# Clustered attention and max-out feed-forward on one core: the exponential left in PSUM for every second score tile

## The chip, the cores and the metric

The kernel runs on one NeuronCore of one Trainium2 chip. The core has a matrix engine (TensorE, PE in the rows; its weight loads are PEld), a vector engine (VectorE, DVE), a scalar engine (ScalarE, ACT), a general engine (GpSimd, POOL) and a queue that issues the transfers (SyncE, SP). SBUF is the working memory of 128 partitions; PSUM is the matrix engine's result memory, 8 banks of 512 float32 values in each partition. POOL does not touch PSUM in this kernel; DVE and ACT read it. The metric is device time of one execution in microseconds (us).

## The reference

Shapes: `q`, `k`, `v` are (4 batches, 8 heads, 768 positions, 64), there are 16 centroids per head, and the feed-forward takes 3072 tokens of 512 through 768 hidden columns.

```python
q_assign = argmax(einsum('bhsd,hcd->bhsc', q_n, c_n), axis=-1)
k_assign = argmax(einsum('bhsd,hcd->bhsc', k_n, c_n), axis=-1)
mask = q_assign[:, :, :, None] == k_assign[:, :, None, :]
scores = where(mask, scale * matmul(q, k.transpose(0, 1, 3, 2)), -1e9)
scores = scores - max(scores, axis=-1, keepdims=True)
attn = exp(scores)
attn = attn / (sum(attn, axis=-1, keepdims=True) + 1e-9)
x = matmul(attn, v)                      # then to [3072, 512]
h = maximum(maximum(x @ w1, x @ w2), x @ w3)
out = h @ w_out
```

## The kernel before

**Precision.** Every float32 operand of a large product is held as two float16 parts, a high half (the rounded value) and a low half (value minus high half). A product is then three matmuls: high by high, high by low and low by high. The inputs are scaled by powers of two first; for queries and keys of a pair of heads the factor to scale the scores back is in a `[128, 1]` tile, `psc`.

**Steps.** A pair is two neighbouring heads; a group is three query tiles of 128 rows. The attention runs in 192 steps, one for each (batch, group, pair, head, query tile): 48 for a batch, 24 for each of its two groups, six for one pair in one group. A step (function `scores`) is this chain:

1. PE (L475, L477) makes a score tile of 128 by 768 float32 in a PSUM buffer called `big`. L475 starts the sum and L477 adds to it; the cluster mask is a part of L477's product.
2. DVE takes the row maximum `mx` (L481), and turns it into `nm`, minus the scaled maximum (L483).
3. ACT makes the exponential `e` in SBUF from PSUM, with `psc` as its scale and `nm` as its bias, and the row sum `rs` (L486); a second small instruction reads the sum out.
4. ACT rounds `e` to the high half in the tile `hl` (L489).
5. The low half, `e` minus high half, is made by DVE in steps 0, 2, 4, ... (even steps) and by POOL in steps 1, 3, 5, ... (odd steps) (L491; `by_pool(step)` is the step's parity).
6. SP issues a transposing transfer of both halves from `hl` to `pt` (L492).

**Buffers.** `big` has three buffers of two banks each. Score tiles, cluster tiles (`cluster_scores`, L419 and L420, read by DVE at L427) and the results of `av` take turns in them. The other two banks are the two buffers of `one`, for the feed-forward. `e` and `hl` have three buffers each.

**Around the steps.** For each pair of each batch, `prep_units` load queries and keys (L360), scale them (L367 and following on DVE), split them into halves (L394 to L396: POOL, ACT, POOL), copy halves between partitions with transfers on SP (L402 to L404) and make the cluster rows (L427 to L456: DVE, POOL, SP). `av` divides and multiplies with `v` after the last step of a pair (L500 to L522). The weights of the feed-forward are loaded and split during the first 46 steps (L195 to L210, L120 paces their loads). The feed-forward of a group (`ffn_units`, L548 to L593) is spread over the 24 steps of the next group; that of the last group comes after all steps.

**What sets the order.** Each unit is given a priority from its step number and an offset; the framework then plays the program through on a model of the engines and writes one fixed order for each engine. On the chip an engine works its own list strictly in that order, and waits at an instruction until the semaphores of its operands and buffers have come. SP likewise issues its transfers in its list's order: a transpose that waits for a low half holds back every transfer behind it.

Of the kernel before, what the change touches and what calls it, by code (L numbers as in the profile page):

```python
# [8 lines left out]
F32 = mybir.dt.float32  # L9
F32R = mybir.dt.float32r  # L10
F16 = mybir.dt.float16
# [4 lines left out]
ALU = mybir.AluOpType  # L16
# [8 lines left out]
def kernel(  # L25
# [324 lines left out]
    masks = {}  # L350

    xin = {}
    psc = {}
    qsc = {}

    def qk_load(b, pr):
# [6 lines left out]
    def qk_scale(b, pr):  # L363

        m2 = sb.tile([P, 2], F32, tag="q_m2", name="q_m2", bufs=2)
        for i, x in enumerate(xin[b, pr]):
            nc.vector.tensor_reduce(m2[:, i : i + 1], x, axis=AX.X, op=ALU.max, apply_absolute_value=True)  # L367
        m = sb.tile([P, 1], F32, tag="q_m", name="q_m", bufs=2)
        nc.vector.tensor_scalar(m, m2[:, 0:1], m2[:, 1:2], 2.0**-10, op0=ALU.max, op1=ALU.max)
        nc.vector.tensor_scalar(m.bitcast(I32), m.bitcast(I32), 0x7F800000, None, op0=ALU.bitwise_and)  # L370
        a = one()[:, 0:P]
        nc.tensor.matmul(a, m.bitcast(BF16)[:, 1:2].broadcast_to([P, P]), ident16, start=True, stop=True)
        p2 = sb.tile([P, 2], F32, tag="q_p", name="q_p", bufs=2)
        nc.vector.tensor_reduce(p2, a.rearrange("p (g d) -> p g d", g=2), axis=AX.X, op=ALU.max)
        r2 = sb.tile([P, 2], F32, tag="q_r", name="q_r", bufs=2)
        nc.vector.reciprocal(r2, p2)
        nc.vector.tensor_tensor(r2, r2, hsel, op=ALU.mult)
        s = sb.tile([P, 1], F32, tag="q_s", name="q_s", bufs=2)
        nc.vector.tensor_reduce(s, r2, axis=AX.X, op=ALU.add)
        n = psc[b, pr] = cpool.tile([P, 1], F32, name=f"psc_{b}_{pr}")  # L380
        nc.vector.scalar_tensor_tensor(n, p2[:, 0:1], SCALE, p2[:, 1:2], op0=ALU.mult, op1=ALU.mult)
        qsc[b, pr] = s

    def qk_split(b, pr):
# [85 lines left out]
    def scores(b, h, qt, pt, g, rs, by_pool):  # L470
        aq, bq, bk, ak = (qkt[b, h // 2][:, j, h & 1] for j in range(4))
        t = big()
        qs = slice(qt * P, (qt + 1) * P)
        for lo, hi in HALF:
            nc.tensor.matmul(t[:, lo:hi], aq[:, qs], ak[:, lo:hi], start=True, stop=False)  # L475
        for lo, hi in HALF:
            last["pe"] = nc.tensor.matmul(t[:, lo:hi], bq[0:K2, qs], bk[0:K2, lo:hi], start=False, stop=True)  # L477
        e = t[:, 0:S]
        p = psc[b, h // 2]
        mx = sb.tile([P, 1], F32, tag="mx", name="mx", bufs=6)  # L480
        nc.vector.tensor_reduce(mx, e, axis=AX.X, op=ALU.max)  # L481
        nm = sb.tile([P, 1], F32, tag="nm", name="nm", bufs=6)
        last["nm"] = nc.vector.tensor_scalar(nm, mx, p, -1.0, op0=ALU.mult, op1=ALU.mult)  # L483
        x = sb.tile([P, S], F32, tag="e", name="e", bufs=3)
        r = rs[:, g, (h & 1) : (h & 1) + 1]
        nc.scalar.activation(x, e, AF.Exp, bias=nm, scale=p, accum_out=r)  # L486
        pace[:] = [r[0:1]]
        hl = sb.tile([P, 2, S], F16, tag="hl", name="hl", bufs=3)
        nc.scalar.copy(hl[:, 0, :], x)  # L489
        eng = nc.gpsimd if by_pool else nc.vector  # L490
        eng.tensor_tensor(hl[:, 1, :], x, hl[:, 0, :], op=ALU.subtract)  # L491
        last["dma"] = nc.sync.dma_start_transpose(out=pt[:, g], in_=hl.rearrange("p a s -> p (a s)"))  # L492
# [3 lines left out]
    def av(b, pr, gi, pts, rs):  # L496

        v = v16[b, pr]
        t = big()
        nc.vector.tensor_scalar_add(rs, rs, 1.0e-9)  # L500
        nc.vector.reciprocal(rs, rs)
        for g in range(G):
            at = 512 + g * P
# [238 lines left out]
```

## Time and profile before

| | us |
|---|---|
| median of three runs | 915.04 (911.82 to 917.27) |
| the profiled execution's own time | 912.16 |
| its span, first to last instruction | 910.4 |
| busy PE / DVE / ACT / POOL | 730.3 / 601.3 / 471.3 / 490.4 |

In the profile's rows, "L491 DVE ... x96 | 123.0, 1281 | 50.9" reads: line 491 on DVE, 96 instructions, together 123.0 us busy, 1281 ns on average, and 50.9 us of idle time of the engine just before them. A timeline row is start in us, duration in us, engine, line, operation, and `output<-inputs` with shapes. A row of the waits is: who waited, for whom, total us, how often, longest us. A row of the table of stretches gives for each engine its busy us and, in brackets, its instructions; then the granted clock of the matrix engine as a share, and the busy share of the transfer engines.

### The profile page before, as it was taken

The page shows a single profiled execution, that of the slowest core. Times are in us where ns is not written, and L with a number is a line of the kernel's source. Part 1 is how long each engine was busy: PE and PEld are TensorE (multiplying, and loading weights), DVE is VectorE, ACT ScalarE, POOL GpSimd, SP SyncE. Part 2 cuts the span into 40 slices and gives each one's busy share as a digit, 9 for nine tenths or more (in the row PEclk, how much of TensorE's full clock was granted, in tenths as well). Part 3 has the DMA queues.
Part 4 walks back from the last instruction along what each step waited for, and adds up shares of the span by engine and source line. Part 5 has one row for each costly group of instructions (what it writes and reads, how often), then busy time and mean ns, then how long its engine had stood idle before and what let it go on. Part 6 is the DMA issues. An engine that isn't in the chain of part 4 may idle for free.

```text
span 910.4 us, 13318 instructions
## 1 busy us (share of the span) xinstructions
PE 730.3 (80%) x4620; PEld 398.1 (44%) x4620; DVE 601.3 (66%) x1138; ACT 471.3 (52%) x785; POOL 490.4 (54%) x471
## 2 busy tenths in 40 slices
PE   2131555686868979999998789999979999999997
PEld 0010222343434435555554455455535655555563
DVE  7785847777789477756868767556785685566110
ACT  2331365685466245566565535665655676566201
POOL 1282276386867556435777564447675754345121
PEclk9998656687977979999999999999999999999999
DMA  6219596897659677786887895789688967667300
GB/s 220 58 22 243 134 222 108 205 197 156 169 136 191 176 162 143 141 157 122 178 180 176 187 207 97 145 148 181 133 184 152 173 121 143 133 121 137 75 1 35
DMA packets 330883, 133.63 MB, mean 147 GB/s; under 512 B 304576, under 2 KB 315712, under 8 KB 330816
## 3 DMA queue, kind: packets, MB, share of 16 engines
q1 hardware_dynamic: 330816, 132.78, 69.4%
q8 instruction: 36, 0.59, 0.3%
q14 instruction: 31, 0.25, 0.1%
HBM read 36.21 MB, written 6.29 MB: 47 GB/s over the span
## 4 chain that ended last, share of the span: by engine, by line
PE 42%; DVE 19%; DMA 13%; POOL 11%; issue 8%; ACT 5%; SPq 1%; POOLq 0%; ACTq 0%; DVEq 0%
PE one L548 19%; PE big L510 8%; PE one L582 6%; DMA pt<-hl 4%; DVE mx L481 4%; DVE hl L491 4%; DMA stage<-in_qk_dram 4%; PE big L475 3%; PE big L477 3%; DMA stage<-in_v_dram 3%; POOL hl L491 3%; PE big L506 2%; POOL qk L396 2%; ACT e L486 2%; ACT hl L489 2%
## 5 line engine op out<-in xcount | busy, mean ns | idle before, releaser
L486 ACT ACTIVATE e<-big,nm,psc 128x768 f32<-128x768 f32 x192 | 189.9, 990 | 214.7 <-DVE nm L483 190.8
L491 POOL TENSOR_TENSOR hl<-e,hl 128x768 f16<-128x768 f32 x96 | 164.6, 1714 | 177.0 <-ACT hl L489 173.3
L548 PE MATMUL one<-x,w16a 128*128 128x384 f16 x1152 | 214.0, 334 | 14.7 <-DVE vf_h L560 4.2
L481 DVE TENSOR_REDUCE mx<-big 128x1 f32<-128x768 f32 x192 | 181.1, 949 | 65.3 <-PE big L477 64.5
L489 ACT CAST hl<-e 128x768 f16<-128x768 f32 x192 | 157.6, 831 | 25.2 <-DMA pt<-hl 22.3
L548 PEld LDWEIGHTS <-w16a 128*128 128x128 f16 x1152 | 113.2, 100 | 100.0 <-issue 31.7
L491 DVE TENSOR_TENSOR hl<-e,hl 128x768 f16<-128x768 f32 x96 | 123.0, 1281 | 50.9 <-ACT hl L489 43.7
L475 PE MATMUL big<-qk 128*128 128x512 f16 (+1 forms) x384 | 104.0, 352 | 57.6 <-ACT e L486 20.3
L510 PE MATMUL big<-pt,v 128*64 128x384 f16 x1152 | 123.0, 349 | 5.6 <-DMA pt<-hl 5.4
L477 PE MATMUL big<-qk 96*128 96x512 f16 (+1 forms) x384 | 106.2, 353 | 22.8 <-DMA qk<-cl_t 18.2
L548 PE MATMUL one<-x,w16b 128*128 128x384 f16 x576 | 104.7, 330 | 4.6 <-DVE vf_h L560 4.4
L510 PEld LDWEIGHTS <-v 128*64 128x64 f16 x1152 | 71.8, 117 | 49.5 <-issue 17.5
L475 PEld LDWEIGHTS <-qk 128*128 128x128 f16 x384 | 34.9, 101 | 109.1 <-issue 66.5
L548 PEld LDWEIGHTS <-w16b 128*128 128x128 f16 x576 | 56.4, 98 | 45.6 <-issue 9.8
L477 PEld LDWEIGHTS <-qk 96*128 96x128 f16 x384 | 40.0, 104 | 55.5 <-DMA qk<-cl_t 17.3
L582 PE MATMUL one<-wo,vf_h 128*128 128x512 f16 x216 | 49.5, 383 | 7.3 <-DVE vf_h L560 3.7
L396 POOL TENSOR_TENSOR qk<-stage,qk 128x768 f16<-128x768 f32 x30 | 50.9, 1708 | 1.9 <-ACT qk L395 1.9
L582 PE MATMUL one<-wo,wf_h 128*128 128x512 f16 x216 | 49.8, 379 | 0.8 <-ACT o L591 0.8
L560 DVE SCALAR_TENSOR_TENSOR wf_h<-one,wf_h 128x384 f32<-128x384 f32 x48 | 26.4, 551 | 35.7 <-PE one L548 32.3
L367 DVE TENSOR_REDUCE q_m<-stage 128x1 f32<-128x768 f32 x32 | 30.1, 947 | 30.1 <-DMA stage<-in_qk_dram 29.9
L506 PE MATMUL big<-ident,rs 128*64 128x128 f32 x384 | 42.0, 312 | 7.6 <-DVE nm L483 7.0
L519 DVE TENSOR_TENSOR xs<-big,xs 128x384 f32<-128x384 f32 x32 | 17.7, 552 | 41.2 <-ACT xs L518 41.2
(140 smaller groups left out, 869.9 us busy)
## 6 DMA issues: line engine op xcount, KB each, us to landing
stage<-in_qk_dram SPq DMA_DIRECT2D x32, 384.0 KB, 4.2
wd<-in_moe_w_dram SPq DMA_DIRECT2D x18, 512.0 KB, 4.8
stage<-in_v_dram SPq DMA_DIRECT2D x24, 384.0 KB, 3.9
out_dram<-o SPq DMA_DIRECT2D x24, 256.0 KB, 2.7
qk<-qk SPq DMA_DIRECT2D x15, 384.0 KB, 4.2
qk<-qk SPq DMA_DIRECT2D x30, 192.0 KB, 3.7
pt<-hl SPq DMA_TRANSPOSE x192, 4.0
wd<-in_moe_w_out_dram SPq DMA_DIRECT2D x6, 512.0 KB, 4.2
```

Source lines behind the costliest of these rows:

```text
L367: nc.vector.tensor_reduce(m2[:, i : i + 1], x, axis=AX.X, op=ALU.max, apply_absolute_value=True)
L396: last["lo"] = nc.gpsimd.tensor_tensor(t[:, AQ, i], x, t[:, BQ, i], op=ALU.subtract)
L475: nc.tensor.matmul(t[:, lo:hi], aq[:, qs], ak[:, lo:hi], start=True, stop=False)
L477: last["pe"] = nc.tensor.matmul(t[:, lo:hi], bq[0:K2, qs], bk[0:K2, lo:hi], start=False, stop=True)
L481: nc.vector.tensor_reduce(mx, e, axis=AX.X, op=ALU.max)
L486: nc.scalar.activation(x, e, AF.Exp, bias=nm, scale=p, accum_out=r)
L489: nc.scalar.copy(hl[:, 0, :], x)
L491: eng.tensor_tensor(hl[:, 1, :], x, hl[:, 0, :], op=ALU.subtract)
L506: nc.tensor.matmul(t[D * i : D * i + D, at : at + P], w, ident, start=True, stop=True)
L510: nc.tensor.matmul(t[D * i : D * i + D, 0:NB], v[:, i, kt, a], pts[i][:, :, c * QT + kt, :], start=(n == 0), stop=(n == len(parts) - 1),)
L548: nc.tensor.matmul(t[:, 0:NB], w16[jt // JA][:, jt % JA, wa, i, ct], x16[b, gi, ct][:, xa, :], start=(n == 0), stop=(n == 3 * CT - 1),)
L582: nc.tensor.matmul(t[:, 0:DM], h16[jt][:, ha, tt * P : (tt + 1) * P], wo16[0][:, jt, wa, :], start=(n == 0), stop=(n == 3 * JT - 1),)
```

## The change

Three things change in a step, and one in `av`.

- **Row maximum.** The reduction and the small instruction after it become one DVE instruction, L480 in the changed file. It multiplies the score tile by `nsc` (minus the old `psc`), writes the product back to the same PSUM tile, and gives out the smallest product of each row as `nm`. The exponential then has the number -1.0 as its scale in place of a `[128, 1]` tile.
- **Exponential.** In odd steps it goes to SBUF as before. In even steps it is written over the scores in PSUM; the cast to the high half and DVE's subtraction read it there. The PSUM buffer is free again after the subtraction, where before it was free after the exponential.
- **Buffers.** `e` has two buffers in place of three, used in odd steps alone; `hl` has four in place of three.
- **`av`.** The addition of 1e-9 to the row sums moves from DVE to ACT.

```diff
-        n = psc[b, pr] = cpool.tile([P, 1], F32, name=f"psc_{b}_{pr}")
-        nc.vector.scalar_tensor_tensor(n, p2[:, 0:1], SCALE, p2[:, 1:2], op0=ALU.mult, op1=ALU.mult)
+        n = nsc[b, pr] = cpool.tile([P, 1], F32, name=f"nsc_{b}_{pr}")
+        nc.vector.scalar_tensor_tensor(n, p2[:, 0:1], -SCALE, p2[:, 1:2], op0=ALU.mult, op1=ALU.mult)
...
         e = t[:, 0:S]
-        p = psc[b, h // 2]
-        mx = sb.tile([P, 1], F32, tag="mx", name="mx", bufs=6)
-        nc.vector.tensor_reduce(mx, e, axis=AX.X, op=ALU.max)
         nm = sb.tile([P, 1], F32, tag="nm", name="nm", bufs=6)
-        last["nm"] = nc.vector.tensor_scalar(nm, mx, p, -1.0, op0=ALU.mult, op1=ALU.mult)
-        x = sb.tile([P, S], F32, tag="e", name="e", bufs=3)
+        last["nm"] = nc.vector.tensor_scalar(e, e, nsc[b, h // 2], 3.0e38, op0=ALU.mult, op1=ALU.min, accum_out=nm)
+        x = sb.tile([P, S], F32, tag="e", name="e", bufs=2) if by_pool else e
         r = rs[:, g, (h & 1) : (h & 1) + 1]
-        nc.scalar.activation(x, e, AF.Exp, bias=nm, scale=p, accum_out=r)
+        nc.scalar.activation(x, e, AF.Exp, bias=nm, scale=-1.0, accum_out=r)
         pace[:] = [r[0:1]]
-        hl = sb.tile([P, 2, S], F16, tag="hl", name="hl", bufs=3)
+        hl = sb.tile([P, 2, S], F16, tag="hl", name="hl", bufs=4)
         nc.scalar.copy(hl[:, 0, :], x)
         eng = nc.gpsimd if by_pool else nc.vector
         eng.tensor_tensor(hl[:, 1, :], x, hl[:, 0, :], op=ALU.subtract)
...
-        nc.vector.tensor_scalar_add(rs, rs, 1.0e-9)
+        nc.scalar.activation(rs, rs, AF.Copy, bias=1.0e-9)
         nc.vector.reciprocal(rs, rs)
```

The lists of all engines are written anew by this. Three places matter later. The first is DVE's list at steps 2 to 5, early in the program. Before (`mx`, `nm`, `big`, `e` and `hl` as above; `q_m`, `cl_t` belong to the preparation of later pairs):

```order
L481 TENSOR_REDUCE mx<-big 128x1
L483 TENSOR_SCALAR nm<-mx,psc_0_163 128x1
L481 TENSOR_REDUCE mx<-big 128x1
L483 TENSOR_SCALAR nm<-mx,psc_0_163 128x1
L481 TENSOR_REDUCE mx<-big 128x1
L491 TENSOR_TENSOR hl<-e,hl 128x768
L483 TENSOR_SCALAR nm<-mx,psc_0_163 128x1
L481 TENSOR_REDUCE mx<-big 128x1
L483 TENSOR_SCALAR nm<-mx,psc_0_163 128x1
L491 TENSOR_TENSOR hl<-e,hl 128x768
L367 TENSOR_REDUCE q_m_645<-stage 128x1
L427 STREAM_TRANSPOSE cl_t<-big 128x768
```

And with the change:

```order
L480 TENSOR_SCALAR big,nm<-big,nsc_0_163 128x768 x2
L488 TENSOR_TENSOR hl<-big,hl 128x768
L480 TENSOR_SCALAR big,nm<-big,nsc_0_163 128x768 x2
L488 TENSOR_TENSOR hl<-big,hl 128x768
L367 TENSOR_REDUCE q_m_617<-stage 128x1
L427 STREAM_TRANSPOSE cl_t<-big 128x768
```

The two subtractions now read `big` in place of `e`, and step 4's row maximum stands behind step 2's subtraction where it stood ahead of it.

The second place is SP's list behind the transposes of steps 0 and 1 (L402, L403 and L404 move the halves of pairs 1 and 2, L360 loads queries and keys, L295 loads `v`). Before:

```order
L402 DMA qk<-qk 64x2x1536
L492 DMA_TRANSPOSE pt<-hl 128x12x128
L402 DMA qk<-qk 64x2x1536
L360 DMA stage<-in_qk_dram 128x768
L403 DMA qk<-qk 64x1536
L492 DMA_TRANSPOSE pt<-hl 128x12x128
L404 DMA qk<-qk 64x1536
L360 DMA stage<-in_qk_dram 128x768
L295 DMA stage<-in_v_dram 128x768
```

And with the change:

```order
L402 DMA qk<-qk 64x2x1536
L489 DMA_TRANSPOSE pt<-hl 128x12x128
L402 DMA qk<-qk 64x2x1536
L360 DMA stage<-in_qk_dram 128x768
L489 DMA_TRANSPOSE pt<-hl 128x12x128
L403 DMA qk<-qk 64x1536
L360 DMA stage<-in_qk_dram 128x768
L404 DMA qk<-qk 64x1536
L295 DMA stage<-in_v_dram 128x768
```

The first transpose shown is step 2's and the second step 4's, both of even steps; the second has moved ahead of pair 1's L403.

The third place is ACT's list at steps 2 to 5 (`v_...` and `qk` are casts of the preparation). Before:

```order
L486 ACTIVATE e,rs<-big,nm,psc_0_163 128x768
L340 CAST v_887<-vf 128x12x64
L489 CAST hl<-e 128x768
L395 CAST qk<-stage 128x768
L486 ACTIVATE e,rs<-big,nm,psc_0_163 128x768
L395 CAST qk<-stage 128x768
L486 ACTIVATE e,rs<-big,nm,psc_0_163 128x768
L489 CAST hl<-e 128x768 x2
```

And with the change:

```order
L483 ACTIVATE big,rs<-big,nm 128x768
L340 CAST v_844<-vf 128x12x64
L483 ACTIVATE e,rs<-big,nm 128x768
L486 CAST hl<-big 128x768
L395 CAST qk<-stage 128x768 x2
L486 CAST hl<-e 128x768
L483 ACTIVATE big,rs<-big,nm 128x768
L486 CAST hl<-big 128x768
```

Step 2's cast, which DVE's subtraction and so the release of its PSUM buffer wait for, now stands behind step 3's exponential.

More of the change, by code (lines that the diff above doesn't have):

```diff
@@ L352 @@
     xin = {}
-    psc = {}
+    nsc = {}
     qsc = {}
```

## The prediction

> **What bounds the kernel now.** I read the page's head, then busy time by stretch, then the chain of work that ended last, then the groups on that chain.
>
> ```profile
> span 910.4 us, 13318 instructions
> 0.00:91.00 91.00, 19.75 (x58) 7.42 (x58) 65.76 (x112) 28.37 (x45) 36.13 (x59) 0.97 0.50 136
> 91.00:364.00 273.00, 197.37 (x1119) 102.60 (x1121) 201.00 (x412) 148.24 (x244) 168.39 (x159) 0.78 0.76 167
> 364.00:862.00 498.00, 470.01 (x3202) 264.17 (x3199) 327.82 (x604) 290.23 (x488) 277.37 (x242) 0.99 0.77 151
> PE 42%; DVE 19%; DMA 13%; POOL 11%; issue 8%; ACT 5%; SPq 1%; POOLq 0%; ACTq 0%; DVEq 0%
> ```
>
> The columns after the stretch are PE, PEld, DVE, ACT, POOL. There are two regimes. From 364 us PE is busy 470.0 of 498 us: only 28 us are open there. Up to 364 us PE is idle 364 - 19.8 - 197.4 = 147 us; DVE is the busiest engine (73%) and the end is set by chains through DVE, POOL, SP and transfers. Little can be won late, much early. Two single instructions stand out in the chain's pieces (start, us, what) and in the low half's line (duration ns least/median/most):
>
> ```profile
> 51.29 15.21 DVE hl L491
> 236.73 5.46 DVE hl L491
> L491 DVE TENSOR_TENSOR hl<-e,hl x96: 915/959/15295, 32.5 to 842.9; 128x768 f16<-128x768 f32 x96
> ```
>
> A subtraction with a median of 0.96 us once took 15.3 us, on the path. POOL's timeline at that time, and SP's behind it:
>
> ```profile
> 49.55 3.39 POOL L210 TENSOR_TENSOR w16a<-wf,w16a 128x512 f16<-128x512 f32 x3
> 52.89 3.24 POOL L396 TENSOR_TENSOR qk<-stage,qk 128x768 f16<-128x768 f32 x2
> 56.07 6.43 POOL L341 TENSOR_TENSOR v<-vf,v 128x768 f16<-128x768 f32 x4
> 62.45 3.24 POOL L396 TENSOR_TENSOR qk<-stage,qk 128x768 f16<-128x768 f32 x2
> 68.60 1.64 POOL L491 TENSOR_TENSOR hl<-e,hl 128x768 f16<-128x768 f32 x1 [0.56 <-ACT hl L489]
> 66.53 1.45 SPq L492 DMA_TRANSPOSE pt<-hl  x1
> 69.66 1.47 SPq L403 DMA_DIRECT2D qk<-qk  x1
> 75.19 0.48 SPq L404 DMA_DIRECT2D qk<-qk  x1
> 76.39 0.39 SPq L295 DMA_DIRECT2D stage<-in_v_dram  x1
> ```
>
> POOL runs two-input instructions without a gap from 49.55 to 65.7 us, and the DVE subtraction ends only after that run: they cannot read SBUF together here. Until then step 2's transpose stands at the head of SP's list, and the moves of pairs 1 and 2 and the loads of `v` behind it, so preparation slips as well.
>
> The Trainium skill, "SBUF — State Buffer", Who interferes with whom, says that a DVE instruction with two SBUF inputs contends with a POOL instruction that reads SBUF, and that the loser waits for that instruction's end. The trace shows the contention, but a wait over eleven POOL instructions; by the page's wait for one instruction (3.24/2 = 1.6 us here) the block, and the first term below, would be about 1 us.
>
> **The low half from PSUM (even steps).** The nearest DVE instruction with one PSUM and one SBUF input:
>
> ```profile
> L519 DVE TENSOR_TENSOR xs<-big,xs x32: 541/553/559, 107.5 to 858.3; 128x384 f32<-128x384 f32 x32
> L491 DVE TENSOR_TENSOR hl<-e,hl 128x768 f16<-128x768 f32 x96 | 123.0, 1281 | 50.9 <-ACT hl L489 43.7
> L481 DVE TENSOR_REDUCE mx<-big 128x1 f32<-128x768 f32 x192 | 181.1, 949 | 65.3 <-PE big L477 64.5
> L367 DVE TENSOR_REDUCE q_m<-stage 128x1 f32<-128x768 f32 x32 | 30.1, 947 | 30.1 <-DMA stage<-in_qk_dram 29.9
> ```
>
> L519 never took more than 559 ns in 32 instances, though POOL is busy over half the time: it is not blocked. For 768 elements, 384 more at (949 - 553)/384 = 1.03 ns (L481 differs only by its reduction), I take 0.95 us. DVE saves 123.0 - 96 x 0.95 = 31.8 us, of which 14.3 and 4.5 are the two long blocks.
>
> What of the first block reaches the end? POOL's run still ends at 65.7 us. L403 moves from 69.66 to about 60: step 2's cast comes after step 3's exponential, its subtraction frees the PSUM buffer at about 52, step 4's scores follow, and their chain of 0.8 (PE), 1.1, 0.9, 0.8, 0.95 with gaps ends near 58; L403 stands behind step 4's transpose. The `v` load at 76.39 needs a stage buffer from POOL's last L396 (65.7): it moves 10 us. The cluster rows of pair 1 follow both. I take -10, between -3 (if they wait for POOL's next low half, which started at 68.60, 2.9 us behind the run) and -14.3. Of the second block I take -3.5 (0 to -4.5). Together **-13.5** (-3 to -18.8).
>
> The remaining excess is 31.8 - 18.8 = 13 us in 94 instructions. L491 on DVE has 3.9% of the chain (last row of this part), 35.5 us; without the two blocks 14.8 us, and of it the share 13/102: **-2** (0 to -13).
>
> ```profile
> by line: PE one L548 19.2%; issue 8.4%; PE big L510 7.9%; PE one L582 5.7%; DMA pt<-hl 4.3%; DVE mx L481 4.2%; DVE hl L491 3.9%; DMA stage<-in_qk_dram 3.6%; PE big L475 3.5%; PE big L477 3.2%; DMA stage<-in_v_dram 2.9%; POOL hl L491 2.8%; P
> ```
>
> **The row maximum in one instruction.** Before it costs DVE 949 + 204 ns:
>
> ```profile
> L483 DVE TENSOR_SCALAR nm<-mx,psc 128x1 f32<-128x1 f32 x192 | 38.2, 204 | 1.9
> L486 ACT ACTIVATION_READ_ACCUMULATOR e<-big,nm,psc 128x1 f32 x192 | 37.2, 194 | 0.0
> L136 DVE MEMSET warm<- 128x1 f32 x1 | 0.1, 59 | 0.8 <-PEq L730 0.8
> L475 PE MATMUL big<-qk 128*128 128x512 f16 (+1 forms) x384 | 104.0, 352 | 57.6 <-ACT e L486 20.3 <-DMA qk<-qk 20.3 <-DVE xs L519 11.8
> L477 PE MATMUL big<-qk 96*128 96x512 f16 (+1 forms) x384 | 106.2, 353 | 22.8 <-DMA qk<-cl_t 18.2 <-DVE qk L458 4.7
> ```
>
> No row shows DVE writing a full tile to PSUM, nor reading out a sum. The pass over 768 elements is 0.95 us by L481; the read-out lies between DVE's smallest instruction, 59 ns, and ACT's read-out, 194 ns. The worst end would be reading and writing one PSUM bank at half speed, 0.95 + 0.80 + 0.19 = 1.94 us. But L477 adds to what L475 wrote, in the same banks, and takes the same time (353 against 352 ns), so PSUM takes a read and a write together, at least from PE. I take 0.95 + 0.15 = 1.10 us, against 1.15. L481 has 4.2% of the chain, 38.2 us, some 40 instances: 40 x -0.05 = **-2** (-6 with 59 ns; +32 at 1.94 us).
>
> **ACT.** From PSUM with no `[128, 1]` operand a copy of 384 takes 476 ns (L518):
>
> ```profile
> L486 ACT ACTIVATE e<-big,nm,psc 128x768 f32<-128x768 f32 x192 | 189.9, 990 | 214.7 <-DVE nm L483 190.8 <-PE big L510 4.1 <-DVE q_r L377 3.7
> L518 ACT COPY xs<-big 128x384 f32<-128x384 f32 x32 | 15.2, 476 | 23.8 <-PE big L510 23.8
> L489 ACT CAST hl<-e 128x768 f16<-128x768 f32 x192 | 157.6, 831 | 25.2 <-DMA pt<-hl 22.3
> L209 ACT CAST w16a<-wf 128x512 f16<-128x512 f32 x12 | 7.3, 616 | 7.3 <-POOL wf L208 7.0
> ```
>
> Per element (831 - 616)/256 = 0.84 ns, so 768 from PSUM would be 476 + 323 = 0.80 us: the even cast saves 0.03 us. The exponential's 0.99 is 0.19 more, with two such operands; one of them goes: 0.90 us, saving 0.09. ACT sheds 192 x 0.09 + 96 x 0.03 = 20 us and gains 32 additions at about 0.2. On the chain (ACT 5%, 45 us, about half of it these two lines) this is a tenth of the exponential's part: **-2** (0 to -5). An ACT write to PSUM no row shows; I take that of SBUF, and hold a loss of 0.1 us each as the other end (10 us of ACT work, at 5% on the path half a microsecond).
>
> **Addition of 1e-9, buffers.**
>
> ```profile
> L500 DVE TENSOR_SCALAR rs<-rs x32: 153/171/1620, 82.3 to 845.6; 128x6 f32<-128x6 f32 x32
> L500 DVE TENSOR_SCALAR rs<-rs 128x6 f32<-128x6 f32 x32 | 13.4, 420 | 7.0 <-ACT e L486 7.0
> ACT hl L489 <- DMA pt<-hl: 22.3, 19, 4.0
> PE big L475 <- ACT e L486: 20.3, 15, 4.0
> ```
>
> L500 has a median of 171 ns and a most of 1620: 13.4 - 32 x 0.17 = 8 us is blocking of the same kind. At DVE's 19% of the chain 13.4 us is worth **-2** (0 to -4). ACT waited 22.3 us for a free `hl`; a fourth buffer takes most of that off, at ACT's 5% plus the steps that wait for the cast, **-2** (0 to -5). `e` has two buffers for 96 odd tiles where it had three for 192; I count nothing for it.
>
> **The price: PSUM held longer.** An even tile's buffer is kept through cast and subtraction, 0.80 + 0.95 us and gaps, about 2.2 us. Behind a late buffer PE's next L475 waits, and behind it in PE's list the feed-forward's L548, for which ACT and DVE wait in turn. Before, PE waited for the exponential's buffer 15 times, 20.3 us. If half of these were even tiles, 7 x 2.2 = 15 us more of PE waiting, but the list is planned anew and most would fall before 364 us, where PE is idle anyway: **+4** (0 to +29).
>
> Sum: -13.5 - 2 - 2 - 2 - 2 - 2 + 4 = -19.5 from the profiled 912.16, 892.7. The profiled execution is 2.9 below the median of the three runs; the same above the sum gives **895 us**.
>
> The Trainium skill, "Perfetto Trace Analysis", Optimizing Scalar/DVE Operations, states about 125 ns of access overhead for DVE on PSUM against 60 on SBUF. L367 (SBUF) and L481 (PSUM) at 947 and 949 ns don't show it; by the page 96 x 65 ns = 6 us more DVE work, an estimate, would make the sum 1 us worse.
>
> **Rivals.**
>
> *DVE paced the early part as a whole.* Steps by stretch, counted by L481:
>
> ```profile
> 91.00:364.00 273.00, 52.70 (x56) 0.78 0.76 167
> 364.00:862.00 498.00, 122.81 (x130) 0.99 0.77 151
> ```
>
> Then the work removed counts fully, not by its share of one chain: between 91 and 364 us DVE loses about a third of 31.8 - 14.3, a third of 13.4 and 56 x 0.05, some 13 us, and before 91 us all 14.3; with the later steps' 3 that is -30, and -5 of ACT and buffers: 877 + 3 = 880, and 875 with the read-out at 59 ns (56 x 0.09 more). For it: DVE's 73%. Against: DVE has 19% of the chain, and transfers and POOL, which do not shrink, 24%.
>
> *Given back.* The first block goes, but the loads and moves were only kept in a queue that is full anyway (transfer engines 76% busy from 91 to 364 us), so -13.5 becomes -6; the buffers cost +8; the rest is hidden: 912 - 6 + 8 - 3 + 3 = 914.
>
> *PSUM becomes the bound: slower.* Three `big` buffers serve scores, cluster tiles and `av`. After 364 us PE is 94% busy, and a wait for a buffer there goes into the time. Each even tile that stops PE by the full 2.2 us costs that; gains of 20 are used up by 9 of 96 even tiles, and 18 give 915 + 20 = 935. For it: 15 such waits already. Against: in the late part a step takes 498/130 = 3.8 us, so three buffers turn over in some 10 us, and a tile's chain with the hold, 0.9 + 1.1 + 0.9 + 0.8 + 0.95 and gaps of 2, is under 7. The Trainium skill, "Perfetto Trace Analysis", Identifying Performance Opportunities (Optimization Strategy), reads the same gap repeated on the busy engine as possible shortage of SBUF or PSUM for the next tile; no such repetition shows here so far.
>
> *It doesn't do what it says:* the lists show the subtraction reading `big`, so that is out; but if PSUM-reading subtractions were blocked too, the first terms vanish: 905.
>
> **How the numbers follow.** Forecast (882 to 909) 0.57; DVE paced 0.14; given back, or blocked all the same (905 to 919) 0.15; slower 0.14. The range is **868 to 915**: it leaves out the slower case and the far end of the DVE case, about 2 in 10. About 0.5% (4.6 us) is what measurement can tell. Faster: 0.57 + 0.14 + a third of 0.15 = 0.76; same 0.11; slower 0.13, since a little of that case lies within the bound.
>
> **What would show it.** Right: L488 on DVE near 0.95 us with a maximum under 1.1; no DVE instruction over 3 us near 50 or 237 us; L403 near 60 us; PE's idle time up to 364 us down by some 15 us. The fused row maximum near 1.1 us with its read-out, the exponential near 0.90. Wrong: L475 waiting for DVE's L488 in many tiles after 364 us and PE busy below 94% there; the fused instruction near 1.9 us; or another DVE instruction with two SBUF inputs caught by POOL's run in place of L491.

## The result, and the profile after

| | before | changed |
|---|---|---|
| median time, us | 914.97 (911.82 to 917.27, 4 runs) | 881.05 (878.53 to 882.03, 4 runs) |
| profiled execution / its span, us | 912.16 / 910.4 | 881.36 / 879.5 |
| ratio to before | | 0.963 [0.959, 0.966] |

The change makes the kernel 34 us faster. The forecast was 895 us with a range of 868 to 915: the sign and the range are right, the gain is 14 us larger than forecast.

The head of the changed kernel's page with its busy time, and the shares of the engines in its chain of work that ended last:

```profile
span 879.5 us, 13242 instructions
PE 724.3 (82%) x4620; PEld 395.3 (45%) x4620; DVE 544.3 (62%) x1106; ACT 456.0 (52%) x817; POOL 460.1 (52%) x471
PE 47%; POOL 15%; DMA 13%; DVE 11%; issue 9%; ACT 3%; SPq 2%; DVEq 0%; POOLq 0%; ACTq 0%
```

Its busy time in the three stretches that the prediction used (PE, PEld, DVE, ACT, POOL):

```profile
0.00:91.00 91.00, 26.70 (x107) 11.77 (x109) 58.93 (x123) 31.71 (x53) 38.98 (x63) 0.81 0.58 159
91.00:364.00 273.00, 207.89 (x1299) 112.00 (x1296) 199.48 (x424) 155.89 (x278) 166.16 (x169) 0.87 0.82 174
364.00:862.00 498.00, 477.03 (x3162) 265.93 (x3161) 285.35 (x560) 266.48 (x485) 253.51 (x237) 0.98 0.73 142
```

Up to 364 us PE is idle 364 - 26.7 - 207.9 = 129 us, where it was 147. DVE's share of the chain fell from 19% to 11%. DVE is busy 57 us less (601.3 to 544.3), ACT 15 us less (471.3 to 456.0), and POOL 30 us less (490.4 to 460.1), although no work of POOL was taken away.

The instructions of a step in the changed kernel (line, engine, operation, count: least/median/most ns, first and last start):

```profile
L480 DVE TENSOR_SCALAR_CACHE_REDUCE big<-big,nsc x192: 979/1018/1027, 25.4 to 812.9; 128x768 f32<-128x768 f32 x192
L480 DVE DVE_READ_ACCUMULATOR big<-big,nsc x192: 83/141/144, 26.4 to 813.8; 128x1 f32 x192
L483 ACT ACTIVATE big<-big,nm x96: 855/875/902, 26.5 to 811.3; 128x768 f32<-128x768 f32 x96
L483 ACT ACTIVATE e<-big,nm x96: 892/902/922, 33.2 to 814.1; 128x768 f32<-128x768 f32 x96
L486 ACT CAST hl<-big x96: 783/799/821, 27.5 to 812.3; 128x768 f16<-128x768 f32 x96
L488 DVE TENSOR_TENSOR hl<-big,hl x96: 914/956/959, 33.2 to 813.8; 128x768 f16<-128x768 f32 x96
```

The subtraction from PSUM takes 956 ns at the median and never more than 959: nothing blocks it. The fused row maximum takes 1018 + 141 = 1159 ns of DVE. ACT's exponential takes 875 ns into PSUM and 902 into SBUF.

SP's timeline of the changed kernel around the place where step 2's subtraction was blocked before, then POOL's (first and last of its run of two-input instructions) and DVE's:

```profile
59.15 0.62 SPq L403 DMA_DIRECT2D qk<-qk  x1
64.77 0.33 SPq L295 DMA_DIRECT2D stage<-in_v_dram  x1
```

```profile
50.18 3.38 POOL L210 TENSOR_TENSOR w16a<-wf,w16a 128x512 f16<-128x512 f32 x3
63.10 3.24 POOL L396 TENSOR_TENSOR qk<-stage,qk 128x768 f16<-128x768 f32 x2
```

```profile
51.66 0.96 DVE L488 TENSOR_TENSOR hl<-big,hl 128x768 f16<-128x768 f32 x1 [2.44 <-ACT hl L486]
55.58 0.96 DVE L488 TENSOR_TENSOR hl<-big,hl 128x768 f16<-128x768 f32 x1 [0.35 <-ACT hl L486]
```

POOL's run of two-input instructions is still there, from 50.2 to 66.3 us. DVE's subtractions of steps 2 and 4 now run in the middle of it in 0.96 us each. The move of pair 1 (L403) is issued at 59.15 us (69.66 before), the load of `v` at 64.77 us (76.39 before).

Where the 34 us come in can be read from the start of each step's first L475 in the profiled executions, counted like all times here from the first instruction. (The recorded expectations count these starts from the zero of the raw trace, 11 us earlier: 89.1 us there is 77.9 here.) The columns are the start of steps 6, 60 and 191, the time from step 60 to 191 and PE's idle time in it, and the median time of all executions; all kernels of the study stand in the table, and the letters are explained below.

| kernel | step 6 | step 60 | step 191 | 60 to 191 | PE idle in it | median time |
|---|---|---|---|---|---|---|
| before | 77.9 | 351.8 | 841.1 | 489.3 | 29.6 | 915.0 |
| before, list 1 / list 2 | 78.3 / 77.9 | 357.6 / 358.3 | 841.3 / 843.5 | 483.7 / 485.2 | 29.8 / 28.4 | 911.0 / 915.6 |
| A: before, step 2 in PSUM | 75.0 | 351.8 | 839.5 | 487.7 | 28.7 | 908.4 |
| B: before, even steps in PSUM | 63.0 | 348.5 | 848.3 | 499.8 | 34.3 | 912.4 |
| C: before, fused maximum | 79.3 | 350.5 | 856.6 | 506.1 | 25.8 | 929.3 |
| C, list 2 | 79.6 | 347.4 | 841.6 | 494.1 | 34.5 | 915.0 |
| **changed** | 65.4 | 323.6 | 812.0 | 488.4 | 22.9 | 881.1 |
| changed, list 1 / list 2 | 64.4 / 64.2 | 329.8 / 324.4 | 810.5 / 799.7 | 480.7 / 475.4 | 27.0 / 26.0 | 880.4 / 869.1 |
| G: changed, two-step maximum | 62.8 | 332.2 | 838.2 | 506.0 | 38.4 | 907.6 |
| G, list 2 | 63.3 | 344.7 | 851.3 | 506.6 | 40.0 | 915.5 |
| H: changed, step 2 in SBUF | 79.1 | 336.6 | 823.2 | 486.6 | 23.1 | 893.6 |
| F: changed, three `hl` | 64.6 | 337.7 | 830.7 | 493.1 | 27.1 | 904.2 |

The changed kernel is 12.5 us ahead at step 6 and 28.2 ahead at step 60; the 131 steps after that add 0.9. Nearly all of the gain lies where the prediction looked for it, before 364 us. Of the growth between steps 6 and 60 about 6 us are idle time of PE (82.7 to 76.8 in that stretch of each kernel) and some 10 its busy time (191.1 to 181.5): the granted clock was 0.83 there, where it was 0.78 before. Whether that clock is a cause of the shorter time or follows from the shorter waits, no run here separates.

### The profile page after: what moved, and what is told of

Same layout as the page of the kernel before. It is cut to its first block, busy times and chain, and to the rows that moved or that the text cites. A ratio compares the mean times of both kernels' runs of the same rounds, so it can differ in the third digit from the quotient of the medians.

```text
span 879.5 us, 13242 instructions
## 1 busy us (share of the span) xinstructions
PE 724.3 (82%) x4620; PEld 395.3 (45%) x4620; DVE 544.3 (62%) x1106; ACT 456.0 (52%) x817; POOL 460.1 (52%) x471
## 4 chain that ended last, share of the span: by engine, by line
PE 47%; POOL 15%; DMA 13%; DVE 11%; issue 9%; ACT 3%; SPq 2%; DVEq 0%; POOLq 0%; ACTq 0%
PE one L545 20%; PE one L579 10%; PE big L507 7%; PE big L475 4%; PE big L477 4%; DMA stage<-in_qk_dram 4%; DMA wd<-in_moe_w_dram 3%; POOL qk L396 3%; DVE big L480 3%; DMA stage<-in_v_dram 3%; POOL hl L488 3%; POOL stage L394 2%; PE big L503 2%; DMA pt<-hl 2%; POOL v L341 1%
## 5 line engine op out<-in xcount | busy, mean ns | idle before, releaser
L480 DVE TENSOR_SCALAR_CACHE_REDUCE big<-big,nsc 128x768 f32<-128x768 f32 x192 | 193.7, 1018 | 80.4 <-PE big L477 79.5
L488 POOL TENSOR_TENSOR hl<-e,hl 128x768 f16<-128x768 f32 x96 | 159.4, 1660 | 149.6 <-ACT hl L486 144.8
L545 PE MATMUL one<-x,w16a 128*128 128x384 f16 x1152 | 210.9, 330 | 10.5 <-ACT wf_h L555 4.8
L483 ACT ACTIVATE big<-big,nm 128x768 f32<-128x768 f32 x96 | 84.0, 875 | 138.2 <-DVE big L480 124.0
L545 PEld LDWEIGHTS <-w16a 128*128 128x128 f16 x1152 | 112.1, 99 | 92.4 <-issue 23.1
L475 PE MATMUL big<-qk 128*128 128x512 f16 (+1 forms) x384 | 103.2, 350 | 42.4 <-ACT e L483 13.5
L507 PE MATMUL big<-pt,v 128*64 128x384 f16 x1152 | 129.5, 341 | 7.5 <-DMA pt<-hl 7.5
L483 ACT ACTIVATE e<-big,nm 128x768 f32<-128x768 f32 x96 | 86.7, 903 | 79.2 <-DVE big L480 63.4
L488 DVE TENSOR_TENSOR hl<-big,hl 128x768 f16<-128x768 f32 x96 | 91.3, 951 | 49.6 <-ACT hl L486 49.3
L486 ACT CAST hl<-e 128x768 f16<-128x768 f32 x96 | 80.1, 834 | 1.6
L545 PEld LDWEIGHTS <-w16b 128*128 128x128 f16 x576 | 56.8, 99 | 50.9 <-issue 15.3
L475 PEld LDWEIGHTS <-qk 128*128 128x128 f16 x384 | 36.1, 102 | 92.9 <-issue 57.2
L486 ACT CAST hl<-big 128x768 f16<-128x768 f32 x96 | 76.7, 798 | 1.8
L518 POOL TENSOR_SCALAR x<-xs 128x384 f16<-128x384 f32 x32 | 16.4, 513 | 75.6 <-DVE xs L516 71.9
L579 PE MATMUL one<-wo,vf_h 128*128 128x512 f16 x216 | 53.9, 380 | 2.0 <-DVE vf_h L557 2.0
```

The costliest lines, as they stand in the source:

```text
L480: last["nm"] = nc.vector.tensor_scalar(e, e, nsc[b, h // 2], 3.0e38, op0=ALU.mult, op1=ALU.min, accum_out=nm)
L483: nc.scalar.activation(x, e, AF.Exp, bias=nm, scale=-1.0, accum_out=r)
L507: nc.tensor.matmul(t[D * i : D * i + D, 0:NB], v[:, i, kt, a], pts[i][:, :, c * QT + kt, :], start=(n == 0), stop=(n == len(parts) - 1),)
L545: nc.tensor.matmul(t[:, 0:NB], w16[jt // JA][:, jt % JA, wa, i, ct], x16[b, gi, ct][:, xa, :], start=(n == 0), stop=(n == 3 * CT - 1),)
L579: nc.tensor.matmul(t[:, 0:DM], h16[jt][:, ha, tt * P : (tt + 1) * P], wo16[0][:, jt, wa, :], start=(n == 0), stop=(n == 3 * JT - 1),)
```

## The experiments

The reason on record was the blocked subtraction. Its rivals were that the new list of orders was simply a better one, that DVE's total work paced the early part, and that something else in the change carried the gain. Each kernel changes the instructions, and so its list is planned anew; a difference of a few microseconds between two kernels can be the list. Four runs measure how much.

**Other lists, same instructions.** `F_LATE` and `AV_LATE` are offsets in the planner's priorities for the feed-forward and for `av`. List 1 is `F_LATE` 0.25, list 2 is `AV_LATE` 2.5:

```diff
-    W_LATE, F_LATE, AV_LATE = -5, 0, 2
+    W_LATE, F_LATE, AV_LATE = -5, 0.25, 2     # list 1
+    W_LATE, F_LATE, AV_LATE = -5, 0, 2.5      # list 2
```

> The kernel before, the same instructions, but the feed-forward's units a quarter of a step later in priority, so that the planner writes other lists from about step 40 on. Theory A (the gain of the change is its cheaper and unblocked instructions; a new list alone is worth a few us): 910 to 920. Theory B (a list's luck is worth 10 us and more here; part of the 34 us is that): outside of 905 to 925 for one of the four kernels of this kind, and the first 36 steps unchanged in each.

> The kernel before with av half a step later in priority: other lists from about step 12 on. Theory A: 910 to 920. Theory B: as likely outside of this as within. In both the block of about 15 us near 51 us stays, since the lists are the same up to there.

> The changed kernel with the feed-forward's units a quarter of a step later in priority: other lists from about step 30 on. Theory A: 876 to 888. Theory B: some 10 to 20 us slower, since the changed kernel's own list would be a lucky one: with the exponentials in PSUM and the row maximum in two instructions only 7 us were left of the gain, and the fused row maximum alone cost 14.

> The changed kernel with av half a step later in priority: other lists from about step 30 on. Theory A: 876 to 888. Theory B: 890 to 905. By both, step 6 begins near 76 us as in the changed kernel.

Measured: before 910.99 (ratio 0.996 [0.993, 0.999]) and 915.63 (1.001 [0.999, 1.003]); changed 880.37 (0.962 [0.959, 0.965]) and 869.06 (0.949 [0.947, 0.951]). Three lists of the old instructions lie within 911 to 916, three of the new within 869 to 882. The gain of the whole change is not a lucky list. A list alone is worth 12 us here, though, and 14 us in C below, so a single-part kernel needs a margin of that size. The changed kernel under list 2 is the fastest of all.

**A: only step 2's exponential in PSUM** (on the kernel before).

```diff
-        x = sb.tile([P, S], F32, tag="e", name="e", bufs=3)
+        x = e if (b, h, qt) == (0, 0, 2) else sb.tile([P, S], F32, tag="e", name="e", bufs=3)
```

> The kernel before, with the exponential of step 2 alone left in PSUM; the other 95 even steps as before. Theory 1 (the subtraction of step 2 was held up only because both its inputs lay in SBUF while POOL ran two-input instructions): it takes 0.95 us in place of 15.3, step 6 begins some 13 us earlier (near 76 us in place of 89.1), and the time falls by 10 to 13 us, to about 903. Theory 2 (the slip was covered, and the gain of the change comes from elsewhere): step 6 begins earlier, but the time stays within 4 us of 915. By either, the rest of the time, from step 48 to step 60 for example (69.9 us before, 58.4 after the change), stays as before unless the new lists alone change it.

Measured: 908.4 us, ratio 0.993 [0.991, 0.995]. The subtractions on DVE in this run, and the longest of them in DVE's timeline:

```profile
L491 DVE TENSOR_TENSOR hl<-e,hl x95: 907/959/13824, 32.7 to 841.2; 128x768 f16<-128x768 f32 x95
L491 DVE TENSOR_TENSOR hl<-big,hl x1: 959/959/959, 50.5 to 50.5; 128x768 f16<-128x768 f32 x1
```

```profile
56.38 13.82 DVE L491 TENSOR_TENSOR hl<-e,hl 128x768 f16<-128x768 f32 x1 [0.85 <-ACT hl L489]
```

Step 2's subtraction, now from PSUM, takes 0.96 us inside POOL's run. Step 4's, still from SBUF, starts at 56.38 inside the same run and is held for 13.82 us. The block moved to the next even step, and step 6 starts only 3 us earlier. Neither expected time came, and the block had not gone. It is the operands that decide, not the step; to take the block off the subtractions, every even step near POOL's run must read PSUM. Of the 7 us by which the median fell the trace shows less than 2 at step 191, and a list alone is worth more.

**B: all even exponentials in PSUM, nothing else** (on the kernel before).

```diff
-        x = sb.tile([P, S], F32, tag="e", name="e", bufs=3)
+        x = sb.tile([P, S], F32, tag="e", name="e", bufs=3) if by_pool else e
```

> The kernel before, with the exponential of all even steps in PSUM and nothing else of the change (row maximum in two instructions, three hl, 1e-9 added on DVE). Theory 1 (the gain is the DVE instructions that are no longer blocked): no subtraction over 1.0 us, and most of the 34 us, about 887. Rival (the fused row maximum and the shorter exponential carry a good part): not under 898.

Measured: 912.41 us, ratio 0.997 [0.995, 1.000]. No subtraction is blocked, but another DVE instruction is: L500, the addition of 1e-9 in `av`, which the change moves to ACT and B leaves on DVE. The subtractions and L500, the longest L500 in DVE's timeline, and POOL's timeline around it (first and last of a run without a gap):

```profile
L491 DVE TENSOR_TENSOR hl<-big,hl x96: 914/956/959, 32.9 to 850.0; 128x768 f16<-128x768 f32 x96
L500 DVE TENSOR_SCALAR rs<-rs x32: 152/172/9901, 68.6 to 852.3; 128x6 f32<-128x6 f32 x32
```

```profile
216.31 9.90 DVE L500 TENSOR_SCALAR rs<-rs 128x6 f32<-128x6 f32 x1
```

```profile
215.06 1.63 POOL L491 TENSOR_TENSOR hl<-e,hl 128x768 f16<-128x768 f32 x1
224.55 1.62 POOL L396 TENSOR_TENSOR qk<-stage,qk 128x768 f16<-128x768 f32 x1
```

PE waits for things that cost it little or nothing before (who waited, for whom: total us, times, longest):

```profile
PE big L475 <- DVE hl L491: 10.4, 7, 3.8
PE big L506 <- DVE rs L501: 18.0, 5, 8.0
```

An instruction of six elements per partition, which takes 0.17 us at the median, is held until POOL's run ends at 226.2 us, and another at 110.4 us for 5.29 us; before, its longest was 1.62. The block has moved once more. L501 stands right behind L500 on DVE, and PE's wait for it in `av` was 0.6 us before. B is 14.9 us ahead at step 6 and still 11.2 at step 37, which starts at 218.4 us; at step 38 it is 1.6 behind, where the changed kernel goes from 15.6 to 16.9 ahead. At step 60 3.3 us are left, and the last 131 steps take 10.5 us longer than before, 4.7 of them idle time of PE. Some 7 us of this late loss can be the choice of executions: B's profiled one is the slowest of its ten, 4.4 us above their median, and that of before is 2.8 below its own.

The part that was meant to carry the gain gives 3 us alone: the "given back" rival, at its price. What took the lead back was in part the blocked L500 and in part PE's wait for the subtraction to release a PSUM buffer, a wait that the kernel before could not have; B does not separate the two, and no kernel was run with the even exponentials in PSUM and the addition on ACT alone. B ran under one list only.

**C: only the fused row maximum** (on the kernel before; the exponentials stay in SBUF; `nsc` takes the place of `psc`, and the plain -1.0 that of the scale tile), and the same under list 2.

```diff
-        mx = sb.tile([P, 1], F32, tag="mx", name="mx", bufs=6)
-        nc.vector.tensor_reduce(mx, e, axis=AX.X, op=ALU.max)
-        last["nm"] = nc.vector.tensor_scalar(nm, mx, p, -1.0, op0=ALU.mult, op1=ALU.mult)
+        last["nm"] = nc.vector.tensor_scalar(e, e, nsc[b, h // 2], 3.0e38, op0=ALU.mult, op1=ALU.min, accum_out=nm)
-        nc.scalar.activation(x, e, AF.Exp, bias=nm, scale=p, accum_out=r)
+        nc.scalar.activation(x, e, AF.Exp, bias=nm, scale=-1.0, accum_out=r)
```

> The kernel before, with the fused row maximum alone; every exponential in SBUF. The fused pass and its read-out are 1.16 us on DVE against 1.15 before, and the exponential is 0.09 us shorter. Theory 1: the block of about 15 us near 51 us stays, and the time is within 5 us of 915. Rival: 12 us or more are gained, since the exponential starts sooner.

> The kernel before with only the fused row maximum, under the other order list. Under the first list it had 929.3, 14 more than before. Theory A, the loss came from the long block of the DVE subtraction (17 us there) and from a list that met it badly, the fused instruction costing nothing itself: under this list within 1% of before, 906 to 924, and some subtraction still over 10 us. Theory B, the fused pass alone is dearer in itself: 925 or more again.

Measured: 929.3 us, ratio 1.016 [1.013, 1.019]; under list 2 915.02, 1.000 [0.998, 1.002]. The subtraction and ACT's wait for a free `hl` in C, and then in C under list 2:

```profile
L488 DVE TENSOR_TENSOR hl<-e,hl x96: 910/958/17027, 32.6 to 858.4; 128x768 f16<-128x768 f32 x96
```

```profile
ACT hl L486 <- DMA pt<-hl: 24.1, 23, 2.4
```

```profile
L488 DVE TENSOR_TENSOR hl<-e,hl x96: 914/958/17025, 32.6 to 843.4; 128x768 f16<-128x768 f32 x96
```

```profile
ACT hl L486 <- DMA pt<-hl: 37.9, 32, 3.7
```

The block is there in both, now 17.0 us. The fused maximum alone gains nothing, and its loss of 14 us under the first list is not repeated under the second, so it is not the instruction's own price. Under list 2 ACT waits 37.9 us for the transfers that release `hl`, where before under list 2 it was 25.1: a sign, not a proof, that tiles that get their row maximum sooner stand before the next limit. Under the first list that wait is 24.1 us, so it does not explain the 14 us. They lie behind step 60 (506.1 us against 489.3), and not in PE's idle time there (25.8 us against 29.6): PE is busy longer with the same matmuls, 480.3 us against 459.7. Why stays open.

**G: the changed kernel with the row maximum in two instructions again**, that is the reverse of the last diff, with the scale factor as the exponential's `[128, 1]` scale; and the same under list 2. Even exponentials in PSUM, four `hl`, and the addition on ACT stay.

> The changed kernel, with the row maximum in two instructions again (and psc as the exponential's scale). Theory 1: within 5 us of the changed kernel, about 881 to 886. Rival: 893 or more, if the fused row maximum carries a good part of the gain.

> The change without its fused row maximum (two instructions again), under the other order list (the late work of the averages starts half a step later), the list that brought the whole change to 869. Theory A, the fused maximum is needed because it ends each tile's row maximum sooner: without it about 900 to 912 again (the kernel in two instructions had 907.6 under the first list), and PE again waits over 8 us for the DVE subtraction to release the scores' buffer. Theory B, the 907.6 was only a bad list: about 872 to 890.

Measured: 907.6 us, ratio 0.993 [0.990, 0.995]; under list 2 915.54, 1.002 [1.000, 1.004]. PE's waits in G (four rows), and in G under list 2 (one row):

```profile
PE big L510 <- DMA pt<-hl: 19.8, 12, 6.2
PE big L475 <- DVE hl L491: 13.8, 7, 3.8
PE big L419 <- DVE hl L491: 10.0, 3, 4.4
PE big L475 <- ACT e L486: 15.6, 10, 5.2
```

```profile
PE big L475 <- DVE hl L491: 24.3, 7, 10.9
```

The same waits in the changed kernel:

```profile
PE big L475 <- ACT e L483: 13.5, 8, 3.6
PE big L475 <- ACT hl L486: 2.8, 1, 2.8
PE big L475 <- DVE hl L488: 0.9, 1, 0.9
```

With the old two-instruction maximum the change loses 26.6 us under its own list and 46.5 under list 2 (915.5 against 869.1): most of its gain and then all of it, both times more than a list was seen to be worth. In both G kernels the steps from 60 to 191 take 506 us, against 488.4 and 475.4 with the fused maximum, and PE is idle 38.4 and 40.0 us in them, against 22.9 and 26.0. (The rest of the difference under list 2 is busy time of PE, 466.6 us against 449.4.) PE waits 13.8 + 10.0 us for the subtraction to release a buffer, under list 2 24.3 in L475; in the changed kernel L475 waits 0.9 us for it in all. The wait of `av` for transposed tiles grows too: 19.8 us in G, 7.5 in the changed kernel.

The fused instruction is not shorter on DVE. What it does can be seen in G's own DVE list, in a piece of its timeline:

```profile
504.06 0.92 DVE L481 TENSOR_REDUCE mx<-big 128x1 f32<-128x768 f32 x1
504.89 0.28 DVE L374 TENSOR_REDUCE q_p<-one 128x2 f32<-128x128 f32 x1
505.09 0.14 DVE L104 TENSOR_SCALAR sc_m<-sc_m 128x1 int32<-128x1 int32 x1
505.15 0.95 DVE L491 TENSOR_TENSOR hl<-big,hl 128x768 f16<-128x768 f32 x1
506.02 0.55 DVE L560 SCALAR_TENSOR_TENSOR wf_h<-one,wf_h 128x384 f32<-128x384 f32 x1
506.48 0.20 DVE L369 TENSOR_SCALAR q_m<-q_m 128x1 f32<-128x1 f32 x1
506.60 0.20 DVE L483 TENSOR_SCALAR nm<-mx,psc 128x1 f32<-128x1 f32 x1
```

Between the maximum (L481) and the small instruction that makes `nm` from it (L483) the list holds five others. From the start of the maximum to the end of `nm` it takes 506.80 - 504.06 = 2.74 us. Worked out over all steps from 60 on, it is 1.84 us before, 1.75 in G, and 1.08 in the changed kernel; over steps 12 to 59, 2.32, 2.35 and 1.07. In 109 of the 192 steps of before, and in 111 of G, it is over 1.5 us; in the changed kernel in none. The fused pass and its read-out were never parted. The exponential, and with an even step everything that holds the PSUM buffer, starts that much sooner. From a tile's first L475 to the release of its buffer, mean over steps 60 to 191, an even and an odd tile added, it is 10.6 us before, 12.7 in B, 12.8 in G and 10.4 in the changed kernel: the hold costs 2.1 us for two tiles, and the change pays it back. Of the 2.4 us between G and the changed kernel 1.3 are the shorter way to `nm` and 0.2 the shorter exponential; the rest are shorter waits between the links. G differs from the changed kernel also by the exponential's second `[128, 1]` operand. G's exponentials, into PSUM and into SBUF:

```profile
L486 ACT ACTIVATE big<-big,nm,psc x96: 943/964/989, 27.0 to 837.6; 128x768 f32<-128x768 f32 x96
L486 ACT ACTIVATE e<-big,nm,psc x96: 978/991/1031, 32.8 to 841.1; 128x768 f32<-128x768 f32 x96
```

They take 89 ns more each than the changed kernel's 875 and 902, 17 us of ACT work in 192 steps; what share of the loss is theirs, these runs do not tell.

**H: the changed kernel with step 2's exponential in SBUF again.**

```diff
-        x = sb.tile([P, S], F32, tag="e", name="e", bufs=2) if by_pool else e
+        x = sb.tile([P, S], F32, tag="e", name="e", bufs=2) if by_pool or (b, h, qt) == (0, 0, 2) else e
```

> The changed kernel, but step 2's exponential goes to SBUF again, so that its DVE subtraction has two SBUF inputs while POOL runs its eleven instructions. Theory A (the prediction's first term, -10, and the 12.6 us by which the changed kernel was ahead at step 6): the block of 13 to 17 us is back, in step 2, and the time is 8 to 13 longer than the changed kernel: 889 to 894. Theory B, what is lost there is made up later: 880 to 884.

Measured: 893.57 us, ratio to before 0.976 [0.972, 0.981], 12.5 us more than the changed kernel. DVE's timeline, and the other 95 subtractions:

```profile
50.96 17.02 DVE L488 TENSOR_TENSOR hl<-e,hl 128x768 f16<-128x768 f32 x1 [0.30 <-ACT hl L486]
```

```profile
L488 DVE TENSOR_TENSOR hl<-big,hl x95: 911/957/960, 32.4 to 825.0; 128x768 f16<-128x768 f32 x95
```

One instruction out of 13 thousand, 16 us longer, costs 12.5 us of the kernel's time. Step 6 starts 13.7 us later than in the changed kernel, and 11.2 us of this are left at step 191. A list can hardly be the cause here: in the traces PE and POOL work through the same order of lines as in the changed kernel, and DVE's and ACT's orders differ in three places each. The first term of the prediction is confirmed by this run, in its place and its size.

**F: the changed kernel with three `hl` buffers.**

```diff
-        hl = sb.tile([P, 2, S], F16, tag="hl", name="hl", bufs=4)
+        hl = sb.tile([P, 2, S], F16, tag="hl", name="hl", bufs=3)
```

> The changed kernel with three hl buffers in place of four. By the prediction's term (-2, bounds 0 to -5) it takes 881 to 886, and ACT's wait for the transfer that releases hl is back at about 20 us. If the fourth buffer carries much of the gain: over 890.

Measured: 904.19 us, ratio to before 0.989 [0.984, 0.993], 23 us more than the changed kernel. Busy time of the engines, ACT's wait, and two of PE's waits:

```profile
PE 730.0 (81%) x4620; PEld 395.1 (44%) x4620; DVE 551.0 (61%) x1106; ACT 457.1 (51%) x817; POOL 460.0 (51%) x471
```

```profile
ACT hl L486 <- DMA pt<-hl: 21.7, 20, 2.8
PE big L475 <- ACT e L483: 19.6, 10, 5.2
PE big L503 <- DVE hl L488: 7.6, 1, 7.6
```

ACT's wait is back at 21.7 us, and the kernel's time rises by about as much, where one list leaves a doubt of up to 14: the orders of DVE, ACT and POOL differ from the changed kernel's in many places. Step 6 starts as early as in the changed kernel, step 60 14 us later, and the steps after that take 4.7 us more. ACT works in its list's order, so a cast that waits for `hl` holds back the next exponential; and an even tile's cast now stands between its exponential and the release of its PSUM buffer, so the transfer that frees `hl` has become a part of the PSUM hold. The even tile's hold over steps 12 to 59 is 9.3 us here and 8.7 in the changed kernel. A fourth `hl` in the kernel before was not run.

## Why the prediction was right, and where it was not

**The two regimes: right.** "Little can be won late, much early": 28.2 of the 29.1 us of lead at step 191 were won before step 60.

**The first block: right in place and size.** The term was -10 of the two blocks' -13.5; H measures 12.5 for the first one. Every step of the argument shows in the trace: POOL's run unchanged, L403 at 59.15 us against "about 60", the `v` load 11.6 us earlier against "10". What the argument left out is that the block moves on to the next DVE instruction that POOL's runs can catch: in A to step 4, in B to L500. The Trainium skill, "SBUF — State Buffer", Who interferes with whom, says that a DVE instruction with at most one SBUF input, outside the modes that use both of its ports, does not contend with POOL; 96 subtractions at 914 to 959 ns in the changed kernel agree. L500 in B has one input and was held 9.90 us; whether it runs in such a mode, no run here shows. The wait for one instruction, which the prediction took from the page, does not hold here: 13.8 and 17.0 us in A and H, like 15.3 before. The second block's -3.5 was not measured by itself.

**The subtraction's duration: right.** 0.951 us against 0.95; 123.0 - 91.3 = 31.7 us of DVE work against 31.8.

**The fused row maximum: the largest error.** The step that failed is "40 x -0.05 = -2". It priced the instruction by its busy time. That term came out at nothing: 193.7 + 26.8 = 220.5 us of DVE, where before it was 181.1 + 38.2 = 219.3. What counts once the exponentials hold PSUM is the time from the start of the maximum to `nm`, 1.84 to 1.08 us late and 2.32 to 1.07 early, since the old pair was parted by other instructions in DVE's list. The timeline of before showed this, and I did not read it. Taken out of the change, it costs 26.6 and 46.5 us (with the exponential's operand and the lists' doubt); put in alone, it gains nothing.

**The fourth `hl`: too small, perhaps by ten times.** The step was the weighting of ACT's 22.3 us of waiting by ACT's 5% of the chain, -2. F measures 23 us, under one list. The weight of one chain was the wrong one, because the wait sits in a list in front of the next exponential, and, with this change, inside the PSUM hold.

**PSUM held longer: right for the whole, for the wrong reason.** The term of +4 assumed that the waits would fall into PE's idle time before 364 us. Without the fused maximum they fall after it too: from step 60 to 191 PE is idle 34.3 us in B and 38.4 in G, where it was 29.6 before. So the mechanism of "PSUM becomes the bound" is real, and "given back" is what B did. In the whole change the hold is paid back: an even and an odd tile hold their buffers 10.4 us, against 10.6 before. How much the hold costs where it is not paid, B does not tell cleanly: by the medians some 12 of its lead of 14.9 us at step 6 are given back, by the profiled executions 22 up to step 191, and the blocked L500 has a part in either. This and the two terms before it are errors of opposite sign that partly cancel, so the sum came out nearer than its terms; that part of the agreement is luck. This hold is not all that decides: under lists 1 and 2 the changed kernel holds its tiles longer, 11.2 and 10.9 us, and is faster still from step 60 on (480.7 and 475.4).

**DVE paced the early part as a whole: its number was nearest, its mechanism wrong.** It gave 880, and 881 was measured, by luck. F saves 50 of the 57 us of DVE work (551.0 us against 544.3 in the changed kernel) and gains 11 of the 34 us; DVE's work saved is not what makes the time.

**ACT: right in sizes.** The exponential 0.875 and 0.902 against 0.90, the even cast 0.798 against 0.80; ACT sheds 20.0 us against 20 in these lines. Its worth in time was not separated.

**The addition of 1e-9: right in kind, its size open.** The term of -2 saw that L500 is blocked in the same way, and priced its 13.4 us of before by DVE's share of the chain. B shows that its worth depends on where L500 meets POOL's runs: there two instances lose 9.90 and 5.29 us. Moving the addition to ACT, and two `e` buffers for three, were not tried alone.

**A rival's price that does not come out.** "It doesn't do what it says" lets the first terms vanish; without -13.5 and the first -2 the sum gives 911, not 905.

**What failed overall** is adding the parts. Taken out singly, the fused maximum, the fourth `hl` and step 2's PSUM tile cost 26.6 + 23.1 + 12.5 = 62 us, while the whole change gains 34; put in singly, the even tiles in PSUM and the fused maximum gain 3 and lose 14 or nothing. Each part moves the limit to the next one: without the block on the subtractions PE waits for PSUM and for L500, and with a sooner `nm` the cast waits for `hl`. The table shows it between steps 6 and 60. With the fused maximum and the fourth `hl` both in place, the lead over before grows there by 15.7 us (8.5 and 13.7 under lists 1 and 2), in H, which has them too, by 16.4. With one of them missing it grows by 0.8 (F) or 4.5 (G), or shrinks by 7.5 (G, list 2), and in B, where both and the addition on ACT are missing, it shrinks by 11.6.

Four things stay open: why C lost 14 us under the first list, what share of G's loss is the exponential's operand, what the addition on ACT is worth, and what in list 2 makes the changed kernel 12 us faster. For the last, the trace shows where: from step 60 to 191 PE is not idle less (26.0 us against 22.9), it is busy 449.4 us in place of 465.5, at a granted clock of 0.99 in place of 0.98.

## What to carry to other kernels

When the end is set by a loop over a few buffers, price an edit by the time from one link of the loop to the next, with all that the engine's list puts between, and not by the instruction's busy time or by its engine's share of one chain. If a change lengthens a buffer's hold, look at what else stands inside the new hold (here a cast that waits for a transfer, and a maximum in two pieces): those must be shortened with it, or the gain is given back. When a block is taken off one instruction, look in the new trace for the next one that it catches. Before a part is judged alone, run the same instructions under two or three lists; here the list alone was worth up to 14 us.

## What the runs showed of the hardware

**The contention costs POOL too.** No POOL work was removed, yet POOL is busy 30 us less. Its scaling of the feed-forward (`vf_h`) and its scaling of `q` and `k`, two rows of before and then the same two of the changed kernel:

```profile
L566 POOL TENSOR_SCALAR vf_h<-vf_h 128x384 f16<-128x384 f32 x24 | 17.3, 721 | 10.9 <-DVE vf_h L560 10.8
L394 POOL TENSOR_SCALAR stage<-stage,q_s 128x768 f32<-128x768 f32 x30 | 30.0, 1012 | 18.0 <-DVE q_s L379 15.2 <-DVE w_s L264 2.8
```

```profile
L563 POOL TENSOR_SCALAR vf_h<-vf_h 128x384 f16<-128x384 f32 x24 | 13.1, 547 | 5.6 <-DVE vf_h L557 5.0 <-DVE sc_m L102 0.5
L394 POOL TENSOR_SCALAR stage<-stage,q_s 128x768 f32<-128x768 f32 x30 | 26.9, 907 | 27.6 <-DVE q_s L379 27.6
```

The same instructions take 547 ns instead of 721 and 907 instead of 1012 on average. The runs show that moving the even exponentials is enough: B, which differs from before in no other instruction, has 460.6 us, and all kernels with them in PSUM have 459.5 to 461.2, while those with them in SBUF have 484.8 to 490.4 (A, with one moved, 479.5). That it is DVE's subtractions that hold POOL up, and not ACT's writing and reading of `e`, is argued and not shown.

**A DVE pass that reads and rewrites 768 float32 per partition in PSUM in place, and gives out a row's minimum**, takes 1018 ns and 141 for the read-out, which overlap by some 80 (1.08 us from start to end); the reduction alone took 949. The feared end of 1.94 us is far off.

**ACT writes PSUM no slower than SBUF:** the same exponential takes 875 ns into PSUM and 902 into SBUF, and the cast 799 from PSUM and 832 from SBUF.
